# Window values for a chunked attention: a DRAM copy in padded groups of four rows, and a later query load

## The chip, the core and the metric

The kernel runs on one core of a Trainium2 chip. The core has five engines that run side by side and wait for each other through semaphores: TensorE (PE in the profile, with PEld for its weight loads), VectorE (DVE), ScalarE (ACT), GpSimd (POOL) and SyncE (SP). Transfers are issued by POOL, SP or ACT and are carried out by 16 DMA engines. The metric is the device time of one execution in microseconds (us), lower is better.

## The reference

Two stages. First a chunked attention over 4 batches, 8 heads, 768 positions and a head size of 64. Each chunk of 32 queries sees 8 memory rows and a window of 56 rows: 16 before the chunk, the chunk, 8 after it, cut at the ends of the sequence.

```python
for c in range(nc):                       # 24 chunks of 32
    l_start = max(0, c_start - 16); r_end = min(S, c_end + 8)
    k_full = concat([mem_k, k[:, :, l_start:r_end]], axis=2)
    v_full = concat([mem_v, v[:, :, l_start:r_end]], axis=2)
    a = softmax(scale * q[:, :, c_start:c_end] @ k_full.T)
    out[:, :, c_start:c_end] = a @ v_full
```

Then the 3072 rows of the result, 512 wide, go through a router with 8 experts: noisy logits, the two best experts for each row, softmax weights over these two, and for each chosen expert `relu(x @ w1[e]) @ w2[e]` with a hidden size of 1024, added up with its weight.

## The kernel before

The attention comes first, then the expert stage. The attention works batch by batch. A batch is three steps of 256 rows (`TP = 3`), so there are 12 steps (`NT`), step `i` belonging to batch `b = i // 3`.

For each batch the inputs come into SBUF by transfers that POOL issues (`load_nat`, line 117), which turn float32 into bfloat16 on the way. Row `p*6 + s` of a head lies on partition `p` in place `s`. From there:

- **Keys and queries** are turned by PE, two heads at a time (`turn`, line 393), into `kT` and `qT`. Four units turn the keys of a batch and four the queries. The units of the next batch are put between the steps of the present one by the table `PLAN`, queries first. DVE and ACT copy each result out of PSUM (line 531 for the first batch, 549 later).
- **Values** need another layout: PE wants, for each chunk, the 8 memory rows and the 56 window rows on 64 partitions, for even heads on partitions 0 to 63 and for odd heads on 64 to 127 (`vb`). Windows overlap and cross partitions, so the values take a way through DRAM. `spread_v` (line 368) lets POOL reorder `vn` into `vp`, in which a partition holds whole rows, the even heads before the odd ones. `window_v` then writes `vp` to the DRAM tile `vd` with one transfer that SP issues (line 374), and reads the windows back with four transfers that POOL issues (line 383): for each half of the heads the first 32 and the last 24 window rows. A partition of `vb` takes 24 pieces of 256 elements, one from each chunk. The memory rows come from `mvn` (line 378). `vd` has 16 rows of zeros before the sequence and 16 behind it, written at the start (line 156).

A step makes the scores (lines 408 and 415), subtracts the maximum (423, 425), takes the exponential on ACT (430), turns the probabilities (436, 439), multiplies with the values (453), divides by the sum (460), turns the rows for the router (470, 472) and makes the logits (480). The rows themselves go to the DRAM tile `xd`, one batch at a time, by a transfer that ACT issues (line 485; the last part by SP). The routing work of finished groups of rows lies between the steps on DVE, POOL and PE.

The order within PE, ACT, DVE and SP is the order of the program (`tc.manual_schedule`), and on POOL everything under `pin` keeps the order of the program too. Around the change POOL's order is: the loads of v, k, q of batch 0; constants; `spread_v(0)`; the memory rows and the window reads of batch 0; the loads of v, q, k of batch 1; `spread_v(1)`; the load of v of batch 2; the memory rows and window reads of batch 1; the loads of q and k of batch 2; and so on. A window read waits for the write of `vd`, and everything that POOL issues later waits behind it. After the window reads of the last batch come the loads of the first three experts.

The expert stage gathers rows from `xd` (line 671), makes the two products (lines 714 and 726), and scatters the sums to the output (line 677). It loads the other experts while it runs.

## Time and profile before

| what | value |
|---|---|
| median of 3 runs | 358.81 us (357.39 to 359.09) |
| the profiled execution | 358.42 us |
| its span, first to last instruction | 356.7 us |
| PE busy | 285.9 us (80%) |
| DVE busy | 170.3 us (48%) |
| ACT, POOL busy | 136.9 and 134.3 us |
| vd written, issue to landing (median of 4) | 9.0 us |
| window reads, issue to landing (median of 8 each) | 13.0 us (384 KB), 13.3 us (288 KB) |
| q, k, v loads, issue to landing (medians of 4) | 18.1, 20.9, 12.1 us |

The profiled time is the span plus 1.7 us around it. In the views, "L383" is line 383 of the kernel. A row of the timeline has the start and the length in us, engine, line, operation, result <- operands, the number of instructions, and in brackets how long the engine had been idle and for what. A row of a DMA queue has packets, MB and the time of its packets as a share of 16 engines; q0 carries what POOL issues, q1 what SP issues, q10 what ACT issues. Shares over 100% mean that packets of one engine overlap. "issue" in a wait means that the profile shows nothing that ended it.

### The profile page before, as it was taken

To read this page: it belongs to the slowest core of one execution; us is meant where nothing else is said; L and a number is where in the kernel's file an instruction comes from. 1 tells how busy PE (TensorE), PEld (TensorE's weight loads), DVE (VectorE), ACT (ScalarE), POOL (GpSimd) and SP (SyncE) were. 2 spreads that over 40 slices of the span, in tenths; PEclk is the share of its full clock that TensorE was granted. 3 is DMA by queue.
4 is the path that set the end of the run, shared out by engine and by line. 5 is a ranking of instruction groups with operands and counts; after the bars stand their busy time and mean duration, and the time that the engine had idled before them with its cause. 6 is when DMAs were issued, how large, how long until landed. Compare 5 with 4: busy or idle time off the path is not lost.

```text
span 356.7 us, 7042 instructions
## 1 busy us (share of the span) xinstructions
PE 285.9 (80%) x2934; PEld 186.3 (52%) x2955; DVE 170.3 (48%) x349; ACT 136.9 (38%) x189; POOL 134.3 (38%) x181
## 2 busy tenths in 40 slices
PE   0356577777847732999999999999999999999991
PEld 0245455666736621865544465664455775565540
DVE  7656456699689885531133302954310334223221
ACT  8813645564645610144322343213243222243310
POOL 6460573354453036706530744332580122201122
PEclk9995655565687865699999999999999999999998
DMA  8999999999999999499999999961289971100012
GB/s 122 235 171 169 245 174 208 251 198 211 247 156 208 253 249 180 106 194 143 178 196 235 209 173 252 159 119 51 87 166 189 208 184 54 53 2 2 25 47 81
DMA packets 49866, 56.97 MB, mean 160 GB/s; under 512 B 16931, under 2 KB 39523, under 8 KB 49828
## 3 DMA queue, kind: packets, MB, share of 16 engines
q0 software_dynamic: 34240, 46.82, 73.2%
q1 hardware_dynamic: 13920, 6.62, 10.9%
q10 hardware_dynamic: 1668, 3.02, 2.4%
q8 instruction: 25, 0.41, 0.5%
q14 instruction: 13, 0.11, 0.1%
HBM read 70.39 MB, written 13.96 MB: 236 GB/s over the span
## 4 chain that ended last, share of the span: by engine, by line
PE 33%; issue 20%; POOL 5%; DVE 4%; DMA 3%; POOLq 1%; ACT 0%; DVEq 0%
PE p_h L714 18%; PE p_y L726 13%; POOL out_dram L677 4%; DMA out_dram<-y,main_dst 1%; DMA xTt<-xt 1%; DMA xt<-xd,main_src 1%; POOL xt L671 1%; DVE w_all L460 1%; PE p_xt L691 0%; POOL w_all L844 0%; POOLq L981 0%; DVE mx L423 0%; DVE sc L425 0%; ACT xT L472 0%; PE ps_o L453 0%
## 5 line engine op out<-in xcount | busy, mean ns | idle before, releaser
L714 PE MATMUL p_h<-xTt,w_all 128*128 128x256 bf16 (+3 forms) x669 | 102.7, 313 | 0.7 <-DVE xTt L692 0.5
L726 PE MATMUL p_y<-w_all,h 128*128 128x512 bf16 x446 | 102.3, 379 | 0.9
L714 PEld LDWEIGHTS <-w_all 128*128 128x128 bf16 x736 | 70.0, 101 | 36.3 <-issue 0.7
L702 ACT ACTIVATE h<-p_h 128x512 bf16<-128x512 f32 (+1 forms) x81 | 44.7, 551 | 95.9 <-PE p_h L714 88.3
L726 PEld LDWEIGHTS <-h 128*128 128x128 bf16 x464 | 45.3, 98 | 51.6
L700 DVE TENSOR_SCALAR h<-p_h 128x512 bf16<-128x512 f32 (+1 forms) x49 | 31.0, 633 | 82.8 <-PE p_h L714 73.7
L677 POOL DMA_INDIRECT out_dram<-y,main_dst x28 | 30.9, 1103 | 87.9 <-DVE y L732 75.4
L732 DVE SCALAR_TENSOR_TENSOR y<-p_y,main_w,y 128x512 f32<-128x512 f32 x28 | 21.0, 750 | 39.2 <-PE p_y L726 32.5
L393 PE MATMUL p_t<-identb,w_all 128*64 128x128 bf16 x384 | 20.6, 288 | 23.0 <-DMA w_all<-in_k_dram 13.4
L671 POOL DMA_INDIRECT xt<-xd,main_src x28 | 27.9, 997 | 24.2 <-DMA xTt<-xt 13.0
L730 ACT ACTIVATE y<-p_y,main_w 128x512 f32<-128x512 f32 x28 | 19.2, 687 | 37.0 <-PE p_y L726 36.0
L393 PEld LDWEIGHTS <-w_all 128*64 128x64 bf16 x384 | 18.1, 155 | 25.2 <-DMA w_all<-in_k_dram 13.9
L439 ACT COPY pT<-p_p 128x1024 bf16<-128x1024 bf16 x12 | 12.1, 1012 | 27.5 <-PE p_p L436 27.5
L383 POOL DMA_DIRECT2D w_all<-vd x16 | 11.8, 747 | 23.8 <-DMA vd<-vp 19.3
L460 DVE TENSOR_TENSOR w_all<-ps_o,rs 128x512 bf16<-128x512 f32 x24 | 15.6, 686 | 8.2 <-PE ps_o L453 7.8
L415 PE MATMUL ps_s<-kT,qT 128*32 128x112 bf16 x384 | 11.6, 276 | 7.2 <-DVE kT L549 5.4
L368 POOL COPY vp<-w_all 128x1536 bf16<-128x1536 bf16 x8 | 11.5, 1469 | 13.2 <-DMA w_all<-in_v_dram 13.2
L430 ACT ACTIVATE pb<-sc 128x1024 bf16<-128x1024 f32 x12 | 12.8, 1063 | 8.9 <-DVE sc L425 8.7
L549 DVE COPY kT<-p_t 64x768 bf16<-64x768 bf16 x12 | 11.5, 955 | 7.9 <-PE p_t L393 7.8
L425 DVE TENSOR_TENSOR sc<-ps_s,mx 128x1024 f32<-128x1024 f32 x12 | 14.7, 1225 | 0.8
L423 DVE TENSOR_REDUCE mx<-ps_s 128x16 f32<-128x1024 f32 x12 | 14.7, 1224 | 0.8 <-PE ps_s L415 0.5
L453 PE MATMUL ps_o<-w_all,pT 128*32 128x128 bf16 x384 | 10.9, 280 | 3.3 <-issue 2.0
(172 smaller groups left out, 284.0 us busy)
## 6 DMA issues: line engine op xcount, KB each, us to landing
w_all<-in_moe_w_dram POOLq DMA_DIRECT2D x16, 1024.0 KB, 20.7
w_all<-in_moe_w_dram POOLq DMA_DIRECT2D x8, 512.0 KB, 13.8
w_all<-in_v_dram POOLq DMA_DIRECT2D x4, 768.0 KB, 12.1
w_all<-in_k_dram POOLq DMA_DIRECT2D x4, 768.0 KB, 20.9
w_all<-in_q_dram POOLq DMA_DIRECT2D x4, 768.0 KB, 18.1
vd<-vp SPq DMA_DIRECT2D x4, 768.0 KB, 9.0
w_all<-vd POOLq DMA_DIRECT2D x8, 384.0 KB, 13.0
w_all<-vd POOLq DMA_DIRECT2D x8, 288.0 KB, 13.3
```

The costliest lines, as they stand in the source:

```text
L393: nc.tensor.transpose(out=p_t[own(par), s, :], in_=src[:, 2 * pair + par, s * D:(s + 1) * D], identity=identb, tile_position=(0, par * 64))
L423: nc.vector.tensor_reduce(out=mx, in_=s3, axis=AX, op=Alu.max)
L425: nc.vector.tensor_tensor(out=sc, in0=s3, in1=bc(mx, KW), op=Alu.subtract)
L460: nc.vector.tensor_tensor(out=xr[:, j, 0:Dm].rearrange("p (h d) -> p h d", h=H), in0=ps_o[:, j].rearrange("p c a d -> p (c a) d"), in1=bc( ...
L671: i = nc.gpsimd.indirect_dma_start(out=xts[key].bitcast(I32), out_offset=None, in_=xd, in_offset=bass.IndirectOffsetOnAxis(ap=ix, axis=0))
L677: i = nc.gpsimd.indirect_dma_start(out=out, out_offset=bass.IndirectOffsetOnAxis(ap=ix, axis=0), in_=y, in_offset=None, bounds_check=N - 1 ...
L700: nc.vector.tensor_scalar(out=out_, in0=in_, scalar1=0.0, scalar2=None, op0=Alu.max)
L702: nc.scalar.activation(out=out_, in_=in_, func=Act.Relu)
L714: nc.tensor.matmul(out=o, lhsT=w(kp * F + f * 128, 128), rhs=x[:, kp], start=(kp == 0), stop=(kp == KP - 1))
L726: nc.tensor.matmul(out=p, lhsT=h[:, (f * n + j) * 128:(f * n + j + 1) * 128], rhs=w(KP * F + f * Dm, Dm), start=(f == 0), stop=(f == FB - 1))
L730: nc.scalar.activation(out=y, in_=p, func=Act.Copy, scale=weight)
L732: nc.vector.scalar_tensor_tensor(out=y, in0=p, scalar=weight, in1=y, op0=Alu.mult, op1=Alu.add)
```

## The change

1. `vd` gets another layout: 8 groups of 4 rows (row within a chunk = 4 g + k), and within a row first the half of the heads (`a`), then the chunk (25 of them, one more than the sequence has, for the window rows that reach over), then the 256 elements of a half row. A group is padded by 256 elements. So the pieces that one partition of `vb` takes lie behind each other in DRAM, 24 x 512 bytes = 12 KB. There are still four reads, now in the order: first 32 rows of the even and the odd heads, then last 24 rows of both.
2. The write of `vp` to `vd` becomes eight transfers on SP, each with 24 partitions and 8 pieces of 512 bytes from each.
3. The values are loaded and spread with 8 rows to a partition on 96 partitions, not 6 rows on 128.
4. The zeros become eight writes in place of four, and are issued behind the loads of the memory keys and values.
5. The queries of batch 0 are loaded behind `spread_v(0)` and ahead of its memory rows and window reads, not at the start.

```diff
@@ -105,26 +105,30 @@
         scol[0] -= n
         return wflat[:, scol[0]:scol[0] + n]
     xrow = [scratch(SO * Dm).rearrange("p (s r) -> p s r", s=SO) for _ in range(2)]
-    vn = scratch(H * SO * D).rearrange("p (h c) -> p h c", h=H)
+    SV = 8
+    VP = S // SV
+    vn = scratch(H * SV * D).rearrange("p (h c) -> p h c", h=H)
     vb = [scratch(2 * NCH * HP * D).rearrange("p (a c w) -> p a c w", a=2, c=NCH) for _ in range(2)][::-1]
     nat = [[scratch(H * SO * D).rearrange("p (h c) -> p h c", h=H) for _ in range(2)] for _ in range(2)]
     assert scol[0] >= 2 * WE
     mvs = w_all[0:B * NM, 0, 0:2 * H * D].bitcast(F32).rearrange("p (h d) -> p h d", h=H)
 
-    vd = [tc.dram_tile([S + CH, Dm], BF16, name=f"vd{i}") for i in range(2)]
+    VR = 4 * 2 * (NCH + 1) * HP * D
+    vd = [tc.dram_tile([CH // 4, VR + HP * D], BF16, name=f"vd{i}")[:, 0:VR].rearrange("g (k a c w) -> g k a c w", k=4, a=2, c=NCH + 1)
+          for i in range(2)]
 
     def load_nat(t, x, b):
         pin(nc.gpsimd.dma_start(out=t, in_=x[b].rearrange("h (p s) d -> p h (s d)", s=SO)))
 
     def load_v(b):
-        load_nat(vn, v, b)
+        pin(nc.gpsimd.dma_start(out=vn[0:VP], in_=v[b].rearrange("h (p s) d -> p h (s d)", s=SV)))
 
     def load_kq(b):
         for x in ((1, 0) if b else (0, 1)):
             load_nat(nat[b % 2][x], (k, q)[x], b)
 
     load_v(0)
-    load_kq(0)
+    load_nat(nat[0][0], k, 0)
 
     actx = ExitStack()
     keep = actx.enter_context(tc.tile_pool(name="keep", bufs=1))
@@ -147,21 +151,20 @@
     make_identity(nc, identb)
     identf = const.tile([NG, NG], F32, name="identf")
     nc.vector.tensor_copy(identf, identb[0:NG, 0:NG])
-    vp = keep.tile([128, H * SO * D], BF16, name="vp")
+    vp = keep.tile([128, SV * Dm], BF16, name="vp")
     lg_all = keep.tile([128, NG, 2 * E], F32, name="lg_all")
     zeros = keep.tile([128, Dm], BF16, name="zeros")
     nc.vector.memset(zeros, 0.0)
-    for i in range(2):
-        for r0, n in ((0, LC), (LC + S, CH - LC)):
-            nc.sync.dma_start(out=vd[i][r0:r0 + n, :], in_=zeros[0:n, :])
-
-
     mks = keep.tile([128, 2, D], F32, name="mks")
     nc.sync.dma_start(out=mks, in_=mem_k.rearrange("b h m d -> (b h m) d").rearrange("(x p) d -> p x d", p=128))
     mkn = keep.tile([128, 2, D], BF16, name="mkn")
     nc.vector.tensor_copy(mkn, mks)
     for b in range(B):
         nc.sync.dma_start(out=mvs[b * NM:(b + 1) * NM], in_=mem_v[b].rearrange("h m d -> m h d"))
+    for i in range(2):
+        for g0, c in ((0, 0), (LC // 4, NCH)):
+            for a in range(2):
+                nc.sync.dma_start(out=vd[i][g0:g0 + LC // 4, :, a, c], in_=zeros[0:LC, 0:HP * D])
     mvn = keep.tile([B * NM, Dm], BF16, name="mvn")
     wgs = keep.tile([128, KP, 2 * E], F32, name="wgs")
     nc.scalar.dma_start(out=wgs[:, :, 0:E], in_=moe_w_gate.rearrange("(kp p) e -> p kp e", p=128))
@@ -366,22 +369,25 @@
     def spread_v(b):
         for par in range(2):
             pin(nc.gpsimd.tensor_copy(
-                out=vp.rearrange("p (s a c d) -> p a c s d", s=SO, a=2, c=HP)[:, par],
-                in_=vn.rearrange("p (c a) (s d) -> p a c s d", a=2, s=SO)[:, par]))
+                out=vp.rearrange("p (s a c d) -> p a c s d", s=SV, a=2, c=HP)[0:VP, par],
+                in_=vn.rearrange("p (c a) (s d) -> p a c s d", a=2, s=SV)[0:VP, par]))
 
     def window_v(b):
         t, o = vb[b % 2], vd[b % 2]
-        nc.sync.dma_start(out=o[LC:LC + S, :].rearrange("(p s) c -> p (s c)", s=SO), in_=vp)
+        for x in range(CH // SV):
+            c0, g = divmod(LC // SV + x, CH // SV)
+            for z in range(2):
+                nc.sync.dma_start(out=o[2 * g + z, :, :, c0:c0 + NCH].rearrange("k a c w -> c (k a) w"),
+                                  in_=vp[x:VP:CH // SV, z * 4 * Dm:(z + 1) * 4 * Dm].rearrange("p (s w) -> p s w", w=HP * D))
         for par in range(2):
             p0 = par * 64
             cols = slice(par * 256, (par + 1) * 256)
             pin(nc.gpsimd.dma_start(out=t[p0:p0 + NM, par], in_=mvn[b * NM:(b + 1) * NM, cols].unsqueeze(1).to_broadcast([NM, NCH, 256])))
-        for par in range(2):
-            p0 = par * 64
-            cols = slice(par * 256, (par + 1) * 256)
-            for r0, n in ((0, CH), (CH, WIN - CH)):
-                pin(nc.gpsimd.dma_start(out=t[p0 + NM + r0:p0 + NM + r0 + n, par],
-                                        in_=o[r0:r0 + S, cols].rearrange("(c k) w -> k c w", k=CH)[0:n]))
+        for x, n in ((0, CH), (1, WIN - CH)):
+            for par in range(2):
+                p0 = par * 64 + NM + x * CH
+                pin(nc.gpsimd.dma_start(out=t[p0:p0 + n, par].rearrange("k c w -> k (c w)"),
+                                        in_=o[0:n // 4, :, par, x:x + NCH].rearrange("g k c w -> g k (c w)")))
 
 
     def turn(b, unit):
@@ -525,6 +531,7 @@
             nc.vector.memset(vb[0][own(par), 1 - par], 0.0)
         nc.vector.tensor_copy(mvn.rearrange("m (a c d) -> m a c d", a=2, c=HP), mvs.rearrange("m (c a) d -> m a c d", a=2))
         spread_v(0)
+        load_nat(nat[0][1], q, 0)
         window_v(0)
         for u in range(2 * HP):
             for o_, i_ in turn(0, u):
```

## The prediction

> **What bounds the kernel now.** I read the span first, then the page's slices of the span.
>
> ```profile
> core 0: 356.7 us, clock 0.867
> PE   0356577777847732999999999999999999999991
> DVE  7656456699689885531133302954310334223221
> DMA  8999999999999999499999999961289971100012
> ```
>
> A slice is 8.9 us. From slice 17 on (about 144 us) PE is full: that is the expert stage, and its end moves with its start. Before that, in the attention, no compute engine is full, and the DMA engines are. The change lies wholly in that first stretch, so the question is which transfers PE waits for there. PE's rows in order of time say it (start, length, what it idled for):
>
> ```profile
> 20.33 2.77 PE L393 MATMUL p_t<-identb,w_all 128*64 128x128 bf16 x48 [3.03 <-DMA w_all<-in_q_dram]
> 32.79 1.04 PE L453 MATMUL ps_o<-w_all,pT 128*32 128x128 bf16 x32 [1.30 <-DMA w_all<-vd]
> 39.77 2.43 PE L393 MATMUL p_t<-identb,w_all 128*64 128x128 bf16 x48 [1.25 <-DMA w_all<-in_q_dram]
> 45.62 2.13 PE L393 MATMUL p_t<-identb,w_all 128*64 128x128 bf16 x36 [3.43 <-DMA w_all<-in_k_dram]
> 61.15 1.04 PE L453 MATMUL ps_o<-w_all,pT 128*32 128x128 bf16 x32 [2.03 <-issue]
> 68.03 1.49 PE L393 MATMUL p_t<-identb,w_all 128*64 128x128 bf16 x24 [2.63 <-DMA w_all<-in_q_dram]
> 98.57 1.46 PE L393 MATMUL p_t<-identb,w_all 128*64 128x128 bf16 x36 [1.44 <-DMA w_all<-in_k_dram]
> ```
>
> The last window read of batch 1 is issued at 47.97 us; its row among the DMA issues ends in the time to landing:
>
> ```profile
> w_all<-vd POOLq DMA_DIRECT2D x1, 288.0 KB, 12.9
> ```
>
> So after the first batch has started, PE loses 1.30 + 1.25 + 3.43 + 2.03 + 2.63 + 1.44 = 12.1 us to late transfers. The row at 61.15 is such a wait too, although it says "issue": the read landed at 47.97 + 12.9 = 60.9 us. All of these transfers are issued by POOL and land one behind the other, so what one of them costs is passed to the next. DVE decides how much of a removed PE wait reaches the end:
>
> ```profile
> 47.16 3.88 DVE L549 COPY kT<-p_t 64x768 bf16<-64x768 bf16 x4 [7.55 <-PE p_t L393]
> 62.25 1.29 DVE L460 TENSOR_TENSOR w_all<-ps_o,rs 128x512 bf16<-128x512 f32 x2 [2.83 <-PE ps_o L453]
> 69.86 0.26 DVE L457 RECIPROCAL rs<-small 128x16 f32<-128x16 f32 x1 [1.04 <-PE small L447]
> 101.77 3.87 DVE L549 COPY kT<-p_t 64x768 bf16<-64x768 bf16 x4
> ```
>
> At 47 and 62 us DVE was idle for longer than PE's wait; at 69.86 for 1.04 us; at 101.77 not at all.
>
> **What the transfers cost.** Rows of the DMA view for six stretches (packets, MB, share of 16 engines). 32 to 39 us, only loads of q, k, v:
>
> ```profile
> q0 software_dynamic: 1867, 1.41, 130.8%
> ```
>
> 52 to 54 us, only window reads, and 22 to 23 us, their beginning in batch 0:
>
> ```profile
> DMA packets 101, 0.33 MB, mean 164 GB/s; under 512 B 21, under 2 KB 21, under 8 KB 101
> q0 software_dynamic: 101, 0.33, 98.9%
> ```
> ```profile
> DMA packets 67, 0.25 MB, mean 254 GB/s; under 512 B 5, under 2 KB 5, under 8 KB 67
> ```
>
> 16 to 18 us, mostly the write of vd; 2 to 3 us, small starting loads; 62 to 64 us, three queues at once:
>
> ```profile
> DMA packets 234, 0.77 MB, mean 385 GB/s; under 512 B 2, under 2 KB 124, under 8 KB 234
> q1 hardware_dynamic: 110, 0.68, 84.7%
> ```
> ```profile
> q1 hardware_dynamic: 355, 0.09, 38.4%
> ```
> ```profile
> q10 hardware_dynamic: 73, 0.45, 54.2%
> q1 hardware_dynamic: 56, 0.29, 36.9%
> q0 software_dynamic: 68, 0.05, 16.6%
> ```
>
> A load packet takes 7 us x 16 engines / 1867 = 60 ns; the 1024 of a q or k load, 64 to an engine, 3.85 us. The window reads of a batch, 2 x 384 and 2 x 288 KB = 1.38 MB, run at 164 GB/s with the engines full: 8.4 us, about 9 with their gaps. The vd write (6 KB runs) has 0.847 x 32 us / 110 = 246 ns a packet, 2.0 us for 128 packets on 16 engines. A small packet of the SP queue (256 B, 2 to 3 us) takes 0.384 x 16 us / 355 = 17 ns. When three queues are busy they pass about equally many packets (73, 56, 68).
>
> **The change, part by part.**
>
> *Window reads (L383).* Every partition now reads one run of 12 KB in place of 24 runs of 512 B. Bounds: 9.0 us a batch as now, and 1.38 MB at 385 GB/s, 3.6 us. I take 4.6 us (300 GB/s): above the 254 of their best stretch and below the 385 of the 6 KB runs, because each DMA still writes 32 or 24 partitions and that row serves 128. Saved: 4.4 us a batch on the queue that everything waits for. The Trainium skill, SBUF — State Buffer, section "Can I just issue two DMAs to hit both halves?", says that two transfers to the two halves of the partitions serialize; by the 218 GB/s that the page gives for 32 partitions the reads would take an estimate of 6.3 us, and no run here shows it.
>
> *vd write (L374).* One DMA with 128 packets of 6 KB becomes eight of 24 x 8 = 192 packets of 512 B: 1536 packets. Price of one: 17 ns for 256 B plus 256 B more at 246 ns per 6 KB (10 ns) = 28 ns, so 2.7 us a batch over 16 engines in place of 2.0: +0.7. Bounds: 2.0 us (the bytes alone) and 60 ns, the load packet, 5.8 us. I take 28, because a plain HW packet is nearer to the HW rows. The Trainium skill, DMA: Bandwidth & Descriptors, "Why a DMA increments its semaphore by 16 and not by 1", says that 24 rows would use 12 engines only; by that it would be an estimate of 3.6 us, and no run here shows the engines. More important is the sharing: at one packet each in turn, 96 write packets beside load packets last 96 x 88 ns = 8.4 us, so vd lands later when loads are queued, while the loads lose only the 2.7 us.
>
> *Eight issues on SP.* An issue takes 0.3 to 0.4 us:
>
> ```profile
> 12.51 68.06 SPq L374 DMA_DIRECT2D vd<-vp  x4
> 127.02 0.32 SPq L485 DMA_DIRECT2D xd<-w_all  x1
> 9.62 2.87 POOL L368 COPY vp<-w_all 128x1536 bf16<-128x1536 bf16 x2 [2.83 <-DMA w_all<-in_v_dram]
> 13.65 1.36 POOL L378 DMA_DIRECT2D w_all<-mvn  x2 [1.17 <-DVE mvn L526]
> 19.97 2.96 POOL L383 DMA_DIRECT2D w_all<-vd  x4 [4.95 <-DMA vd<-vp]
> ```
>
> Eight are about 3 us; SP has nothing else between the four writes and 127 us, so only vd's landing feels it. The eight zero writes (four before) go behind mem_k and mem_v, 3 us before the first spread ends: nothing.
>
> *spread_v (L368).* 96 partitions x 2048 elements a copy in place of 128 x 1536: 2.87 x 4/3 = 3.83 us, +1.0 a batch. It is hidden behind the queue of loads in batches 1 to 3 and on the path in batch 0. While POOL copies (77.34 to 80.2), one DVE row takes 2.49 us that elsewhere takes 0.19:
>
> ```profile
> 77.34 2.88 POOL L368 COPY vp<-w_all 128x1536 bf16<-128x1536 bf16 x2
> ```
> ```profile
> 77.77 2.49 DVE L307 TENSOR_TENSOR facts<-ii 128x6 bf16<-128x6 f32 x1
> 105.67 0.19 DVE L307 TENSOR_TENSOR facts<-ii 128x8 bf16<-128x8 f32 x1
> ```
>
> So a copy that is 1.0 us longer can hold DVE up to 1 us longer in the batch where DVE is full; or nothing, if the copy moves off it. I take nothing and keep 1 us for the range.
>
> *v load*: the same bytes in 768 runs of 2 KB in place of 1024 of 1.5 KB: nothing, as the loads already move 1.41 MB of bf16 in 7 us, 201 GB/s, and twice that in f32.
>
> *q of batch 0.* Its issue goes from 3.45 us to behind the spread: 9.62 + 3.83 = 13.5, data from about 15.3 (an estimate: 0.9 us to issue it and as much to start). Its 64 packets an engine now share with the vd write: 64 x 88 ns = 5.6, plus 0.8 to be reported: 21.7 us in place of 20.3. The first scores slip by 1.4 us. The constants that it is moved behind on POOL merely start 0.9 us earlier. vd lands when both are through, 15.3 + 3.85 + 2.7 + 0.8 = 22.6 (19.9 before). The mvn rows (L378) and the reads stand behind it on POOL; the reads start at 24.0 and end at 28.6 in place of 32.7. Behind them on POOL and in the queue are v, q, k of batch 1, so all of these come about 4 us earlier, less 0.7 for the longer vd write beside k and 0.3 for gaps: k at 42.5 instead of 45.6, 3.1 us.
>
> *The sum.* The 1.4 us of the start is taken up by the waits of 1.30 and 1.25 that vanish. k of batch 1: 3.1 us, in full, as DVE idled 7.55. Windows of batch 1: by then two read savings less two longer writes; they end about 55, PE is ready for them at 59.1 - 3.1 = 56: the wait of 2.03 goes, DVE idled 2.83. q of batch 2: the 2.63 goes, but DVE gives back only its 1.04 and a bit: 1.2. k of batch 3: 1.44 on PE, nothing, DVE was busy. Late next is DVE, which from 66 us on has few gaps. Sum 3.1 + 2.0 + 1.2 = 6.3 us. The profiled execution took 358.42 us (span 356.7), 0.4 below the median of the runs, 358.81: 352.1 there, 352.5 as a median.
>
> **The rivals.** A measurement of this kernel tells about 0.5% (1.8 us) from no change.
>
> 1. *Reads half mended.* Each DMA fills only 32 or 24 partitions and they follow each other at half of the 385 GB/s: 7.1 us, 1.9 saved a batch. Reads of batch 0 end at 31.1, k of batch 1 gains 0.6, the windows 1.8, q 0.8: 3.2, so 355.6 us. For it: 4 KB read packets at 164 GB/s with full engines do not look like a cost per run. Against it: 254 GB/s for 1 us. The Trainium skill's page named at the reads speaks for this one.
> 2. *Reads as slow as now* (the length of the run was never the limit): 9.0 us. In batch 0 they end at 33.0, 0.3 late, and with the longer write k of batch 1 is 1.3 late: 360.1. Against it as above.
> 3. *The small writes are dear* (slower). At 60 ns a packet q of batch 0 lands at 15.3 + 64 x 120 ns + 0.8 = 23.8 and vd at 15.3 + 3.85 + 5.8 + 0.8 = 25.8, the reads end at 31.8, and k of batch 1, beside 5.8 us of writes (3.8 more), lands 32.7 - 31.8 - 3.8 - 0.3 = 3.2 late. With 0.5 more in the next batches, 362.5 us. It decides from the packet price p at which 32.7 - (25.9 + 96 p) and the rest, 192 p in all against 8.45 us, cancel: 44 ns. Against it: 17 ns at 256 B.
> 4. *ACT is held* (slower). ACT issues the write of xd itself:
>
> ```profile
> 57.76 0.37 ACTq L485 DMA_DIRECT2D xd<-w_all  x1
> 50.96 0.91 POOL L117 DMA_DIRECT2D w_all<-in_k_dram  x1 [1.32 <-DMA w_all<-in_v_dram]
> vd<-vp SPq DMA_DIRECT2D x4, 768.0 KB, 9.0
> ```
>
> The second row shows an issue that waits for an earlier, unrelated load to land. With eight writes in place of one, the xd issue could come to wait for one of them, 9.0 us from issue to landing, some 6 us after ACT gets there, in one batch, and 2 in the next: 358.8 - 6.3 + 8 = 360.5 or more. Against it: the order of the issues may stay as it is, xd first.
>
> **How the numbers follow.** Forecast 0.47 (own range 349 to 356); rival 1 0.13 (355.6); rival 2 0.14 (360.1); rival 3 0.19 (362.5); rival 4 0.07 (360.5). Faster: 0.47 + 0.13 = 0.60; same: rival 2 and a little of the others, 0.16; slower: 0.24. The range goes from 348.5 (reads at their lower bound, 1 us a batch more, and the 2.63 and 1.44 of PE counted in part) to 362.5, which holds the rivals but for the worse half of the third; the 1 us of DVE lies inside.
>
> **What would show it.** Right: 12 KB or 4 KB read packets with a DMA rate near 300 GB/s or more in a stretch of reads only; SP's small packets at some 28 ns; the first q rows of PE near 21.7 and those of k of batch 1 near 42.5; no PE wait before L453 near 56. Wrong: a write packet of 45 ns or more, a q row past 23 us, a read rate still at 164, ACT idle before L485.

## The result and the profile after

The changed kernel takes 371.44 us (median of 4 runs, 369.12 to 372.46) against 358.91 us for the kernel before beside it (357.39 to 359.09): ratio 1.035, 95% interval 1.0293 to 1.0406. It is 12.5 us slower; 352.5 us was predicted, at most 362.5. The profiled execution took 372.46 us, its span 370.9. Here and below a ratio counts the runs of a kernel that lie within 1.5% of its fastest; where that leaves many out, the ratio of the medians of all runs stands beside it.

From the page of the changed kernel: the slices of the DMA engines, the groups of the window reads and of the spread (busy us, mean ns of one | idle time before them and what ended it), and the issues of the write (32 in place of 4).

```profile
DMA  8879995995996999969999999961169992100012
...
L389 POOL DMA_DIRECT2D w_all<-vd x16 | 8.7, 551 | 54.1 <-DMA vd<-vp 53.9
L371 POOL COPY vp<-w_all 96x2048 bf16<-96x2048 bf16 x8 | 14.9, 1904 | 12.1 <-DMA w_all<-in_v_dram 12.1
vd<-vp SPq DMA_DIRECT2D x32, 96.0 KB
```

The row of nines in the DMA slices has holes now (5 and 6). POOL stood 53.9 us at the four batches' window reads, waiting for the write of `vd`. The same wait among POOL's waits in the kernel before (us in total, times, longest) was 19.3 us in three batches. For the reads of batch 1 the view names no cause for the 4.4 us that POOL idled before them; with these it is 23.7.

```profile
POOL w_all L383 <- DMA vd<-vp: 19.3, 3, 8.9
```

SP's issues of the write, with their shortest, median and longest duration in ns and their first and last start, in the kernel before and in the changed one:

```profile
L374 SPq DMA_DIRECT2D vd<-vp x4: 319/334/355, 12.5 to 80.2; - x4
```
```profile
L380 SPq DMA_DIRECT2D vd<-vp x32: 750/753/2898, 13.8 to 101.2; - x32
```

PE's rows in order of time answer to those of the prediction:

```profile
23.17 2.77 PE L399 MATMUL p_t<-identb,w_all 128*64 128x128 bf16 x48 [5.46 <-DMA w_all<-in_q_dram]
36.04 1.04 PE L459 MATMUL ps_o<-w_all,pT 128*32 128x128 bf16 x32 [1.71 <-DMA w_all<-vd]
47.36 1.20 PE L399 MATMUL p_t<-identb,w_all 128*64 128x128 bf16 x36 [1.15 <-DMA w_all<-in_k_dram]
69.97 1.04 PE L459 MATMUL ps_o<-w_all,pT 128*32 128x128 bf16 x32 [9.62 <-DMA w_all<-vd]
80.95 2.13 PE L399 MATMUL p_t<-identb,w_all 128*64 128x128 bf16 x36 [1.96 <-DMA w_all<-in_k_dram]
96.45 0.63 PE L459 MATMUL ps_o<-w_all,pT 128*32 128x128 bf16 x32 [2.43 <-DMA w_all<-vd]
109.60 1.20 PE L399 MATMUL p_t<-identb,w_all 128*64 128x128 bf16 x36 [3.11 <-DMA w_all<-in_k_dram]
157.04 1.86 PE L721 MATMUL p_h<-xTt,w_all 128*128 128x128 bf16 x16 [0.52 <-DVE xTt L699]
```

The last row is the first product of the expert stage; before, it stood at 144.14:

```profile
144.14 1.86 PE L714 MATMUL p_h<-xTt,w_all 128*128 128x128 bf16 x16 [0.52 <-DVE xTt L692]
```

So 12.9 of the 14.2 us by which the span grew were lost ahead of the expert stage. The windows of batch 0 were 3.2 us late (36.04 against 32.79), those of batch 1 already 8.8 (69.97 against 61.15), and the largest single wait, 9.62 us, stands there.

What POOL did about the reads of batches 1 and 2 shows how the wait is passed on (start, length, idle time before):

```profile
26.97 2.17 POOL L389 DMA_DIRECT2D w_all<-vd  x4 [10.96 <-DMA vd<-vp]
44.42 1.31 POOL L385 DMA_DIRECT2D w_all<-mvn  x2
58.39 1.64 POOL L389 DMA_DIRECT2D w_all<-vd  x3 [12.66 <-DMA vd<-vp]
60.86 0.96 POOL L121 DMA_DIRECT2D w_all<-in_q_dram  x1
87.40 2.17 POOL L389 DMA_DIRECT2D w_all<-vd  x4 [18.56 <-DMA vd<-vp]
```

The load of q of batch 2 (60.86), and that of k behind it, stand behind the reads. In four stretches just ahead of the reads the DMA engines had nothing left to do; columns are the window, its length, PE, PEld, DVE, ACT and POOL busy, PE's clock, DMA share, GB/s:

```profile
26.00:28.20 2.20, 1.47 (x45) 1.18 (x43) 1.21 (x3) 0.14 (x1) 1.23 (x3) 1.00 0.00 0
56.50:59.60 3.10, 3.10 (x64) 2.73 (x64) 2.95 (x5) 1.12 (x2) 1.21 (x3) 0.50 0.02 3
86.60:88.60 2.00, 2.00 (x36) 1.83 (x28) 1.39 (x2) 0.52 (x1) 1.20 (x3) 0.50 0.01 0
111.20:113.40 2.20, 1.59 (x28) 1.14 (x28) 2.15 (x4) 2.15 (x3) 1.18 (x3) 0.50 0.00 0
```

### The profile page after: what moved, and what is told of

Its sections match the earlier page's. It is cut to its first block, busy times and chain, and to the rows that moved or that the text cites. A ratio compares the mean times of both kernels' runs of the same rounds, so it can differ in the third digit from the quotient of the medians.

```text
span 370.9 us, 7112 instructions
## 1 busy us (share of the span) xinstructions
PE 284.3 (77%) x2955; PEld 183.8 (50%) x2955; DVE 172.7 (47%) x349; ACT 136.7 (37%) x189; POOL 134.7 (36%) x181
## 3 DMA queue, kind: packets, MB, share of 16 engines
q1 hardware_dynamic: 19904, 6.62, 10.8%
## 4 chain that ended last, share of the span: by engine, by line
PE 32%; issue 19%; POOL 5%; DVE 3%; DMA 3%; POOLq 1%; ACT 1%; DVEq 0%; ACTq 0%
PE p_h L721 17%; PE p_y L733 13%; POOL out_dram L684 3%; DMA out_dram<-y,main_dst 1%; POOL xt L678 1%; DMA xTt<-xt 1%; DVE w_all L466 1%; DMA xt<-xd,main_src 1%; PE p_xt L698 0%; PE p_list L355 0%; POOLq L988 0%; POOL w_all L851 0%; ACT xT L478 0%; ACT pT L445 0%; PE p_p L442 0%
## 5 line engine op out<-in xcount | busy, mean ns | idle before, releaser
L733 PE MATMUL p_y<-w_all,h 128*128 128x512 bf16 x464 | 103.7, 379 | 0.0
L399 PE MATMUL p_t<-identb,w_all 128*64 128x128 bf16 x384 | 19.7, 277 | 26.1 <-DMA w_all<-in_k_dram 16.1
L399 PEld LDWEIGHTS <-w_all 128*64 128x64 bf16 x384 | 17.0, 147 | 28.1 <-DMA w_all<-in_k_dram 16.8
L389 POOL DMA_DIRECT2D w_all<-vd x16 | 8.7, 551 | 54.1 <-DMA vd<-vp 53.9
L466 DVE TENSOR_TENSOR w_all<-ps_o,rs 128x512 bf16<-128x512 f32 x24 | 15.5, 686 | 15.4 <-PE ps_o L459 14.8
L459 PE MATMUL ps_o<-w_all,pT 128*32 128x128 bf16 x384 | 9.6, 258 | 14.9 <-DMA w_all<-vd 13.8
L371 POOL COPY vp<-w_all 96x2048 bf16<-96x2048 bf16 x8 | 14.9, 1904 | 12.1 <-DMA w_all<-in_v_dram 12.1
L436 ACT ACTIVATE pb<-sc 128x1024 bf16<-128x1024 f32 x12 | 12.8, 1064 | 13.8 <-DVE sc L431 13.7
L431 DVE TENSOR_TENSOR sc<-ps_s,mx 128x1024 f32<-128x1024 f32 x12 | 14.7, 1225 | 0.8
L429 DVE TENSOR_REDUCE mx<-ps_s 128x16 f32<-128x1024 f32 x12 | 14.7, 1223 | 0.7 <-PE ps_s L421 0.4
L556 DVE COPY kT<-p_t 64x768 bf16<-64x768 bf16 x12 | 11.5, 954 | 7.5 <-PE p_t L399 7.4
L459 PEld LDWEIGHTS <-pT 128*32 128x32 bf16 x384 | 7.3, 114 | 15.3 <-issue 15.1
## 6 DMA issues: line engine op xcount, KB each, us to landing
w_all<-in_v_dram POOLq DMA_DIRECT2D x4, 768.0 KB, 10.6
```

Of the source, the lines that this page charges most:

```text
L371: pin(nc.gpsimd.tensor_copy(out=vp.rearrange("p (s a c d) -> p a c s d", s=SV, a=2, c=HP)[0:VP, par], in_=vn.rearrange("p (c a) (s d) -> p ...
L399: nc.tensor.transpose(out=p_t[own(par), s, :], in_=src[:, 2 * pair + par, s * D:(s + 1) * D], identity=identb, tile_position=(0, par * 64))
L459: nc.tensor.matmul(out=ps_o[r * CH:(r + 1) * CH, j, pair], lhsT=pT[:, j * HP + pair, r * CH:(r + 1) * CH], rhs=vb[b % 2][:, :, (tp * 2 + j ...
L466: nc.vector.tensor_tensor(out=xr[:, j, 0:Dm].rearrange("p (h d) -> p h d", h=H), in0=ps_o[:, j].rearrange("p c a d -> p (c a) d"), in1=bc( ...
L733: nc.tensor.matmul(out=p, lhsT=h[:, (f * n + j) * 128:(f * n + j + 1) * 128], rhs=w(KP * F + f * Dm, Dm), start=(f == 0), stop=(f == FB - 1))
```

## The experiments

The theory at the start, W: the write in eight transfers of small packets lands late, POOL stands at the window reads meanwhile, and the load queue behind POOL runs dry. The rival, Q: the later queries of batch 0 are the loss. The experiments ran on other chips than the result, where the kernel before took 360 to 364 us, so ratios against that kernel on the same chip are compared, and beside them the start of the first p_h row (the attention's end, 157.04 above). That row is of one execution of each kernel. All times are of kernels that differ from the changed kernel or from the kernel before by the edit named; of longer edits the main lines are shown.

### The parts alone: queries, write, number of issues

Queries of batch 0 at the start again, everything else as changed:

```diff
-    load_nat(nat[0][0], k, 0)
+    load_kq(0)
...
-        load_nat(nat[0][1], q, 0)
```

> The changed kernel with the queries of batch 0 loaded at the start again; all else stays changed. Theory W (the vd write lands late, because its 1536 small packets take turns with the queued loads, POOL stands at the window reads until it has landed, and behind POOL the load queue runs dry): the start gains 1 to 3 us, the later batches stay as they are: 368 to 371 us. Rival Q (the late queries and the dead time they leave at the start are the loss): 361 us or less.

Measured: 370.72 us, ratio 1.0221 [1.0158, 1.0284], first p_h row 153.90. So the layout with its write loses 2.2% without the queries' part.

The other way round, the kernel before with nothing but the later queries:

```diff
-    load_kq(0)
+    load_nat(nat[0][0], k, 0)
...
         spread_v(0)
+        load_nat(nat[0][1], q, 0)
```

> The kernel before with only the queries of batch 0 moved behind the spread. Theory W: they land 2 to 3 us later and most of it is met again in the waits for the windows and the next keys: 359 to 361.5 us. Rival Q: 367 us or more.

Measured: 363.54 us, ratio 1.0018 [0.9981, 1.0055]. Batch 0's first q row starts at 23.50 us there, 3.2 later than in the kernel before, and the end does not feel it. Alone, the later queries are not the cause. To the changed kernel they add what lies between 1.0221 and 1.035, about 1.3% (the two ratios are from different chips), 3.1 us in the first p_h row.

The changed kernel with the copy written by one transfer of 96 runs of 8 KB, with late and with early queries:

```diff
-        for x in range(CH // SV):
-            c0, g = divmod(LC // SV + x, CH // SV)
-            for z in range(2):
-                nc.sync.dma_start(out=o[2 * g + z, :, :, c0:c0 + NCH].rearrange("k a c w -> c (k a) w"),
...
+        nc.sync.dma_start(out=vflat[b % 2][0:S * Dm].rearrange("(p c) -> p c", p=VP), in_=vp[0:VP])
```

(`vflat` is the tile of `vd` as one row.)

> The changed kernel with vd written by one transfer of 96 runs of 8 KB a batch, and the zeros by one for the unwritten rest: the window reads keep their 12 KB runs and byte count but find the values in the wrong places, so the attention computes on misplaced values. Theory W: the write is back at 2 us of engine time and lands in 7 to 10 us, so the time falls below the kernel before, 352 to 357 us. Rival Q: 364 us or more, since the start is untouched. If the reads on their few partitions are the loss: 367 or more.

> The one-write kernel (vd written by one transfer of 8 KB runs, so the values lie in wrong places and the attention computes on them) with the queries of batch 0 loaded at the start again. What is left of the change is the 96-partition values and the reads with 12 KB runs. If the 12 KB reads save 4 us of queue a batch as the prediction took, and only the late queries hid it: ratio to the kernel before 0.975 to 0.99. If the reads save engine time but land no earlier, because they lie on few engines each: 0.995 to 1.01.

Measured: 366.03 us, ratio 1.0084 [1.0042, 1.0127], with late queries; 360.8 us, ratio 0.9826 [0.977, 0.9881] (medians of all runs: 0.992), with early ones. POOL's wait at the reads in the second one's page, and its first p_h row:

```profile
L385 POOL DMA_DIRECT2D w_all<-vd x16 | 8.7, 551 | 20.7 <-DMA vd<-vp 18.9
```
```profile
143.69 1.86 PE L716 MATMUL p_h<-xTt,w_all 128*128 128x128 bf16 x16 [0.51 <-DVE xTt L694]
```

The wait is back at 18.9 us. How much the reads gain is less sure. The ten runs with early queries spread from 354.83 to 364.58 us, and the ratio 0.9826 (6.3 us) rests on the four lowest of them; by the medians of all runs the gain is 2.9 us (360.8 against 363.69). In the row, runs in the layout before on the same chip stood at 146.95 (spread on 96 partitions, below) and 148.18 (late queries), 3.3 and 4.5 us behind; this profiled execution took 364.12 us, above its median. So the gain of the reads is 3 to 6 us. With late queries the expectation of W, 352 to 357 us, failed: 366.03 lies in Q's range. Beside a large write the later queries cost about what the reads gain. From large write to small packets, the same row goes from 143.69 to 153.90, 10.2 us.

The kernel before with its write, still in 6 KB packets, cut into eight transfers:

```diff
-        nc.sync.dma_start(out=o[LC:LC + S, :].rearrange("(p s) c -> p (s c)", s=SO), in_=vp)
+        for p in range(0, 128, 16):
+            nc.sync.dma_start(out=o[LC + p * SO:LC + (p + 16) * SO, :].rearrange("(p s) c -> p (s c)", s=SO), in_=vp[p:p + 16])
```

> The kernel before with its vd write cut into eight transfers of 16 partitions, the packets still 6 KB. If the eight issues on SP, some 0.4 us each, make the write late: ratio 1.01 or more. If it is the 512-byte packets that take turns with the loads: within 0.5% of the kernel before.

Measured: 367.84 us, ratio 1.0118 [1.0034, 1.0202]. Eight issues have a price of their own, without small packets: POOL stood 44.9 us at the reads (23.7 before), and the first p_h row came at 154.03, 6 to 7 us behind the two rows named above and as late as that of the changed kernel with early queries. SP's waits show one reason: in the middle of a batch's eight it stood for an unrelated transfer of ACT's.

```profile
POOL w_all L384 <- DMA vd<-vp: 44.9, 4, 14.4
```
```profile
SPq L375 <- DMA xd<-w_all: 15.6, 2, 9.0
```

Four transfers of 16 pieces in place of eight of 8, without padding, queries early:

```diff
-            for z in range(2):
-                nc.sync.dma_start(out=o[2 * g + z, :, :, c0:c0 + NCH].rearrange("k a c w -> c (k a) w"),
-                                  in_=vp[x:VP:CH // SV, z * 4 * Dm:(z + 1) * 4 * Dm].rearrange("p (s w) -> p s w", w=HP * D))
+            nc.sync.dma_start(out=o[2 * g:2 * g + 2, :, :, c0:c0 + NCH].rearrange("g k a c w -> c (g k a) w"),
+                              in_=vp[x:VP:CH // SV].rearrange("p (s w) -> p s w", w=HP * D))
```

> The changed kernel with queries early, without padding, and the copy written by four transfers of 24 partitions with 16 runs of 512 B, instead of eight with 8 runs: the same packets in half as many issues. Theory W in the form that the packets' turns beside the loads are the cost: first to last write packet still 10 to 15 us, ratio 1.02 to 1.04. If the number of issues is the cost (each waits for earlier ones to land): first to last 5 to 8 us, ratio 1.00 to 1.01.

Measured: 370.91 us, ratio 1.0313 [1.0196, 1.043] (medians of all runs: 1.024); the write's packets of batch 1 took 9.9 us from first to last, of batch 2 14.8. Half the issues mend nothing.

Half the values in 512-byte packets, half in 4 KB runs, eight transfers:

```diff
+        for g in range(4):
+            nc.sync.dma_start(out=vt[b % 2][2 * g + 1, 0:S * Dm // 8].rearrange("(p c) -> p c", p=VP // 4),
+                              in_=vp[g * VP // 4:(g + 1) * VP // 4, 4 * Dm:8 * Dm])
```

> The changed kernel with batch 0's queries loaded at the start, eight writes a batch as in the changed kernel, but four of them carry half of the values in 512 B packets (768 a batch instead of 1,536) and four carry the other half in 96 runs of 4 KB, to other places (those values come to lie in wrong places of the copy, so attention works on misplaced values). If the number of small packets sets the write's length: first to last write packet 6 to 8 us instead of 11 to 15, ratio between the runs with all small and with one large write, 1.000 to 1.010. If it is the eight issues: as with all small, 1.015 to 1.025. If the load queue bridges a write of 7 us without running dry: 0.98 to 0.99.

Measured: 371.61 us, ratio 1.0236 [1.0129, 1.0343], first p_h row 152.58; 10 to 13 us from first to last write packet. Half the small packets cost as much as all of them. Neither the number of issues nor the number of packets alone sets the loss. The small-packet transfers of these two runs have 24 rows each, like those of the changed kernel.

### What else was new: spread, padding, where the transfers are issued

The values loaded and spread on 96 partitions, rows unpadded as before, one large write, reads in 512-byte pieces:

```diff
+        nc.sync.dma_start(out=o[LC // 4:(LC + S) // 4, :].rearrange("(p z) r -> p z r", z=SV // 4),
+                          in_=vp[0:VP].rearrange("p (z r) -> p z r", z=SV // 4))
...
+                pin(nc.gpsimd.dma_start(out=t[p0:p0 + n, par],
+                                        in_=o[x * CH // 4:x * CH // 4 + S // 4].rearrange("(c g) (k a w) -> g k a c w", g=CH // 4, k=4, a=2)[0:n // 4, :, par]))
```

> The values' loading and spread on 96 partitions alone: values are loaded and spread as in the changed kernel (96 partitions, eight rows each), but the DRAM copy has rows of all heads one behind the other without padding, is written by one transfer of 96 runs of 8 KB, and is read in 512 B pieces; batch 0's queries are loaded at the start. Theory W (the slow write in eight transfers of 512 B packets holds POOL at the reads and the load queue runs dry) makes this the kernel before in all that counts: ratio 0.995 to 1.010, write first to last packet 3 to 6 us, reads 12 to 15 us a batch. Rival S (the spread on 96 partitions, 1.9 us a call instead of 1.4, and the v load of 96 partitions are themselves dear): ratio 1.02 or more with the same waits.

Measured: 364.05 us, ratio 1.0043 [1.0, 1.0087]. Load and spread on 96 partitions cost next to nothing.

One large write, early queries, no padding:

```diff
-    vt = [tc.dram_tile([CH // 4, VR + HP * D], BF16, name=f"vd{i}") for i in range(2)]
+    vt = [tc.dram_tile([CH // 4, VR], BF16, name=f"vd{i}") for i in range(2)]
```

> One large write as in the earlier run of that kind, queries early, but no padding behind each group of four rows (the reads' 32 or 24 partitions are then one even stride). The values come to lie in wrong places of the copy, so attention works on misplaced values; the work in time is the same. If the gain of 1.7% came from the 12 KB runs alone: ratio 0.977 to 0.990, reads 6 to 8 us a batch. If the padding (the split into groups of four rows, and so the spread over the engines) is what makes the reads fast: reads 10 us or more, ratio 0.995 to 1.005.

Its whole time, 1174 us, tells nothing of the attention: with these misplaced values the expert stage runs far longer. The first line of its page and its first p_h row:

```profile
span 1168.0 us, 12986 instructions
```
```profile
144.25 1.87 PE L716 MATMUL p_h<-xTt,w_all 128*128 128x128 bf16 x16 [0.51 <-DVE xTt L694]
```

Up to that row it is the padded one (143.69) within 0.6 us; the reads of its four batches took 7.6, 12.8, 16.0 and 15.2 us from first to last packet, the padded ones 6.8, 10.6, 12.7 and 10.2. So the long runs make the gain in the row. The padding shortens the reads, but by that row little comes of it.

Loads of keys and queries moved ahead of the window reads on POOL, to keep the queue filled:

```diff
+        if between is not None:
+            between()
         for x, n in ((0, CH), (1, WIN - CH)):
...
-                window_v(b + 1)
-                if b + 2 < B:
-                    load_kq(b + 2)
+                window_v(b + 1, (lambda: load_kq(b + 2)) if b + 2 < B else None)
```

> The changed kernel with POOL issuing the key and query loads of the batch after next ahead of the window reads, so that the load queue is not empty while POOL waits for the vd write. Theory W: two empty stretches of 3 to 5 us of the DMA engines vanish, 362 to 366 us, but the write, which now always has company, lands later still. Rival Q: no change, 370 to 372. If only the landing of the write counts and not the empty queue: 371 or more.

Measured: 375.45 us, ratio 1.0247 [1.0152, 1.0342] (medians of all runs: 1.036): not clearly better than 1.035, and not the 362 to 366 us of W. Its PE waits, in an execution of 377.19 us:

```profile
PE ps_o L461 <- DMA w_all<-vd: 24.6, 3, 15.9
```

The filled queue pushed the write back: first to last packet 20.8 us in batch 1, where the changed kernel had 12.3.

The window reads issued by SP, in the kernel before and in the changed kernel with early queries:

```diff
-                pin(nc.gpsimd.dma_start(out=t[p0 + NM + r0:p0 + NM + r0 + n, par],
+                nc.sync.dma_start(out=t[p0 + NM + r0:p0 + NM + r0 + n, par],
```

> The kernel before with the window reads issued by SP, so that POOL no longer stands behind the vd write and the loads of the next batches are queued without a pause. If POOL standing there costs time in the kernel before too: ratio 0.98 to 0.995. The rival: the load queue of the kernel before never runs empty, so nothing is won, and the reads with 512-byte packets now take turns with the loads and land later: 1.00 to 1.02.

> The changed kernel with the queries of batch 0 at the start and the window reads issued by SP behind the eight writes. If the empty load queue behind POOL's wait is what the slow write costs: ratio 0.99 to 1.01, against 1.022 with the reads on POOL. If it is the late landing of the values themselves: 1.02 or more.

Measured: 376.57 us, ratio 1.0357 [1.028, 1.0434], and 388.19 us, 1.0645 [1.0535, 1.0755]. The first is slower than either theory had it; the second lies where the late landing was to put it. With POOL free to load ahead, the reads are what comes late. PE's waits for the windows, first in the kernel before with its reads on SP, then in the changed one:

```profile
PE ps_o L453 <- DMA w_all<-vd: 25.7, 3, 12.8
```
```profile
PE ps_o L459 <- DMA w_all<-vd: 42.4, 4, 19.8
```

The eight writes issued by POOL, behind the loads in one queue:

```diff
-                nc.sync.dma_start(out=o[2 * g + z, :, :, c0:c0 + NCH].rearrange("k a c w -> c (k a) w"),
+                pin(nc.gpsimd.dma_start(out=o[2 * g + z, :, :, c0:c0 + NCH].rearrange("k a c w -> c (k a) w"),
```

> The changed kernel with batch 0's queries loaded at the start, the eight writes of the values' copy issued by POOL (behind the loads of the next batch in POOL's own queue) instead of by SP. Theory W, in the form that the write is slow because its 512 B packets take turns with the loads' packets on another queue: in one queue they follow each other, first to last write packet 3 to 6 us instead of 11 to 15, the engines stand empty for 2 to 4 us a batch at most, PE's waits for the windows shrink to below 3 us, ratio 0.98 to 1.00. Rival N (512 B write packets are dear wherever they are queued): first to last 10 us or more, ratio 1.02 to 1.04 as with SP. Rival I (the issuing of eight such transfers is the cost): POOL busy 0.7 to 1.5 us more for each, 6 to 12 us a batch, ratio 1.03 or more.

Measured: 371.9 us, ratio 1.0302 [1.0228, 1.0377]. POOL's rows for batch 1:

```profile
42.37 4.34 POOL L380 DMA_DIRECT2D vd<-vp  x7
50.37 0.62 POOL L380 DMA_DIRECT2D vd<-vp  x1 [3.67 <-DMA w_all<-in_v_dram]
53.90 2.18 POOL L389 DMA_DIRECT2D w_all<-vd  x4 [1.65 <-DMA vd<-vp]
```

The wait at the reads is short now (1.65 us here), but POOL spends 11.5 us from the first write to the first read, and the loss is the same. Another queue is no cure. In the trace these writes are 192 packets of 4 KB a batch and not 1536 of 512 bytes, so this run does not test small packets in one queue.

### Taking the loss apart: packets or standing?

Reads that need not wait, because they take the input of the values in place of the copy:

```diff
-                                        in_=o[0:n // 4, :, par, x:x + NCH].rearrange("g k c w -> g k (c w)")))
+                                        in_=v[b].rearrange("h s d -> (h s d)").rearrange("(r c) -> r c", c=NCH * HP * D)[par * CH:par * CH + n]))
```

> The changed kernel with batch 0's queries loaded at the start, where the window reads (same number, same 12 KB runs, same destinations) take their data from the input of the values instead of from the copy, so that POOL need not wait for the copy's write. The eight writes of 512 B packets are still made, beside the loads as before. Values come to lie in wrong places of the windows (attention works on misplaced values), so the MoE's lists differ a little; the start of the MoE's first p_h row is compared beside the time. Theory W (POOL stands at the reads, the load queue runs dry): without the wait the attention is back at what one large write gave, first p_h row at 142 to 147 us and ratio 0.975 to 0.995. Rival B (1,536 small packets a batch beside the loads take the loads' time, waiting or not): first p_h row at 151 to 155 us, ratio 1.01 to 1.03.

Measured: 384.88 us, ratio 1.0599 [1.0518, 1.0681], first p_h row 166.39. Neither theory had this. POOL's wait had only moved, to the next spread, which needs `vp` free:

```profile
POOL vp L371 <- DMA vd<-vp: 51.5, 3, 18.6
```

With the queue full the write took 26 to 28 us from first to last packet in batches 0 to 2. Three stretches of the DMA view, each with a write of the same 0.79 MB (q1) beside loads (q0; packets, MB, share of 16 engines): 46.5 to 74.5 us of this kernel, 45 to 57.5 us of the changed kernel, 40 to 45 us of the kernel before.

```profile
q0 software_dynamic: 2886, 3.71, 84.0%
q1 hardware_dynamic: 1632, 0.79, 14.5%
```
```profile
q0 software_dynamic: 1116, 1.13, 57.6%
q1 hardware_dynamic: 1632, 0.79, 26.2%
```
```profile
q0 software_dynamic: 758, 0.57, 79.0%
q1 hardware_dynamic: 144, 0.79, 38.3%
```

In the changed kernel the write is done after 12 us; the loads beside it run out on the way, and none of them is a read of the input in 12 KB packets, as 112 of the 2886 are.

The same with two `vp` in turn, so that nobody waits for the write, and without the writes:

```diff
-    vp = keep.tile([128, SV * Dm], BF16, name="vp")
+    vps = [vp0, keep.tile([128, SV * Dm], BF16, name="vp")]
```

> As the run whose window reads take the input, and the eight writes a batch are left out altogether (nothing of the values' copy is written but its zero rows; attention works on misplaced values). This is what is left of the changed kernel without the write. If the write is the whole loss: first p_h row at 138 to 145 us, ratio 0.955 to 0.985. If something else in the changed kernel is slow (the reads of 12 KB runs beside the loads, the spread on 96 partitions): first p_h row at 148 us or more, ratio above 1.0.

> As the run whose window reads take the input, with the eight writes of 512 B packets a batch, and with two buffers for the spread values in turn, so that POOL waits for the write neither at the window reads nor at the next spread (it waited 51.5 us at the spread there); attention works on misplaced values. Theory W (the cost is POOL's standing, the packets beside the loads cost little): first p_h row at 138 to 147 us and within 3 us of the run without the writes, ratio 0.96 to 0.99. Rival B (the small packets take the loads' time, turn by turn, waiting or not): first p_h row at 150 us or later, 8 us or more behind the run without the writes, ratio 1.01 or more.

Measured: without writes 356.59 us, ratio 0.9791 [0.9705, 0.9878], first p_h row 139.86; with writes that nobody waits for 365.65 us, ratio 1.0077 [1.0029, 1.0125], row at 148.56. The writes cost 8.7 us though nobody waits for them, so W, in which they cost little, falls in this form; the row itself lies between the ranges of W and B. But these reads were of float32 input, turned into bfloat16 on the way. In the trace their packets have 12 KB, not about 1 KB as the next text has it, but one takes about 1 us, where those of the changed kernel take 0.6 to 0.8. Hence the last pair, with reads of a small bf16 copy:

```diff
-                                        in_=v[b].rearrange("h s d -> (h s d)").rearrange("(r c) -> r c", c=NCH * HP * D)[par * CH:par * CH + n]))
+                                        in_=vz[0:n // 2].unsqueeze(1).to_broadcast([n // 2, 2, NCH * HP * D])))
```

> In the two runs before, the window reads took the input, which is float32 and is turned into bfloat16 on the way; so they were not the 12 KB runs that their expectations named, but packets of about 1 KB. Here the reads take a small bf16 copy (16 rows of 12 KB, written once, in batch 0, by one transfer of 24 runs of 8 KB; two partitions share a row), so they are 12 KB runs and wait for nothing after batch 0. The eight writes a batch in 512 B packets are made, from two buffers in turn, and nobody waits for them. Attention works on misplaced values. If POOL's standing is about half of the loss, as the run with two buffers suggests: first p_h row 4 to 7 us ahead of the changed kernel with early queries (153.90), 147 to 150. If it is the whole loss: at 144 or before. If the packets alone are the loss: at 152 or later.

> As the run with the small copy, without the eight writes (attention works on misplaced values). First p_h row at 135 to 140 us, since the run without writes and with slow reads was at 139.86. Its distance to the run with the writes is the price of 1,536 small packets a batch that nobody waits for: 2.7 us a batch by the price of 28 ns a packet on 16 engines, 10.8 us in all; 7 to 10 us by the distance of the two runs before (8.7). Its distance to the kernel with one large write and early queries (143.69) is the whole price of a large write, wait included: 4 to 8 us.

The expert stage again ran over a millisecond with these values, so only the part up to the first p_h row counts. With writes, without writes:

```profile
149.35 1.86 PE L726 MATMUL p_h<-xTt,w_all 128*128 128x128 bf16 x16 [0.52 <-DVE xTt L704]
```
```profile
135.65 1.86 PE L721 MATMUL p_h<-xTt,w_all 128*128 128x128 bf16 x16 [0.52 <-DVE xTt L699]
```

This divides the attention's end, with early queries: 135.65 with no write; 143.69 with one large write and its wait (+8.0); 149.35 with small packets that nobody waits for (+13.7, where 7 to 10.8 was expected); 153.90 with small packets and POOL standing at the reads (another 4.6). So of the 10.2 us between large write and small packets, at least 5.7 are what the write takes from the loads, and up to 4.6 POOL's standing. The division is rough. Each row is of one execution, the last pair ran on a chip whose kernel before took 359.65 us, 0.7 to 1.1% less than beside the other two, and the pair before it has the write at 8.7 us in place of 13.7. Each share may be off by some 2 us, the first by more.

No version with all values in their places beat the kernel before.

## Why the prediction was wrong, step by step

*What bounds the kernel* was read rightly: transfers in the attention; 12.9 of the 14.2 us of the span lie there.

*Window reads: right in kind, priced too well.* From issue to PE, batch 0: 19.97 to 32.79 before, 12.8 us; 26.97 to 36.04 after, 9.1. Saved 3.8 us (4.4 predicted). Their packets took 7.2, 9.1, 7.0 and 6.7 us from first to last in the four batches, not 4.6. Rival 1 had 7.1, but counted its gain from 9.0 us where the kernel before took 12.8 from issue to use. With one large write the reads gained 3 to 6 us at the end. The Trainium skill's rule for the two halves of the partitions (SBUF — State Buffer, "Can I just issue two DMAs to hit both halves?"), by which 6.3 us was estimated, is nearer to the trace's 7 us than the forecast was.

*vd write, its own time: about right.* 28 ns a packet was taken, 10.8 us for four batches on 16 engines. The two pairs of runs with and without the small packets give 8.7 and 13.7 us, 23 and 36 ns a packet. The large write cost 8.0 us for four, the 2.0 us a batch predicted, but with its waits in it. By the second pair the extra is 5.7 us in place of 2.8; the first pair has no run with a large write.

*vd write, its landing: the step that failed.* "At one packet each in turn, 96 write packets beside load packets last 96 x 88 ns = 8.4 us, so vd lands later when loads are queued, while the loads lose only the 2.7 us" was worked out for batch 0 and then dropped: for batch 1 the prediction has "two read savings less two longer writes; they end about 55", as if POOL had not to wait for that landing. PE had the windows of batch 1 at 69.97. Spread 1 ended at 43.4 us, the write landed at 58.4, and POOL, with the loads of q and k of batch 2 behind it, stood until then (12.66 us), while the queue emptied (56.5 to 59.6). By the division above, this standing is up to 4.6 us of the loss.

The 8.4 us were too short as well, by the number of engines and by the length of a turn. The 1632 packets of a batch's write are 1536 of data and 96 more, 12 for each of the eight transfers; the large write's 144 are 128 and 16. That agrees with the rule of the Trainium skill, DMA: Bandwidth & Descriptors, "Why a DMA increments its semaphore by 16 and not by 1", by which 24 rows use 12 engines. Then an engine has 136 of the packets and not 96. The stretch of 70 to 76 us, batch 2's write beside a full load queue, gives the turn:

```profile
q0 software_dynamic: 1209, 0.93, 98.7%
q1 hardware_dynamic: 665, 0.32, 27.2%
```

On twelve engines that is a write packet in 6 us x 12 / 665 = 108 ns, where 88 was taken. 136 x 108 ns = 14.7 us is an estimate from these rows; the write took 15.4 us from first to last packet. In the 28 us shown above, whose loads include the 12 KB reads, a turn took 206 ns in the same way.

*Eight issues: wrong in size.* 0.3 to 0.4 us was taken from an issue of 128 long runs; one of 24 x 8 short ones took 0.75, some up to 2.9. Eight lasted 9.6 and 10.3 us in batches 0 and 1 and 6.5 in batch 2, not 3. That "only vd's landing feels it" was true and mattered.

*Rival 3, dear small writes,* had the right sign. Its threshold of 44 ns was too high, since POOL's standing was left out of batches 1 to 3; at 23 to 36 ns the kernel already lost.

*q of batch 0: too cheap in company.* The q row was predicted at 21.7 and came at 23.17, past the mark of 23 that the prediction named as wrong. By itself the move cost nothing (1.0018), with the slow write about 1.3%, with one large write 1.8% by the medians of all runs (366.03 of 362.24 us against 360.8 of 363.69). The wait of 1.30 us that was to vanish and take it up is still there, 1.71 us at 36.04.

*Spread, v load, zeros: right.* Two copies of 1904 ns, 3.81 us a batch (3.83 predicted), and nothing measurable at the end (1.0043). *Rival 4:* ACT was not held; it was SP that stood for ACT's transfer, and only in runs with eight issues (0.2 us in the changed kernel itself).

*What stays open.* The parts measured do not quite make up the whole: 10.2 us for the write and 3.1 for the later queries, less 3 to 6 for the reads, are 7 to 10 of the 12.9 us, from rows of different chips.

Open too is how even the turns are. The Trainium skill, DMA: Bandwidth & Descriptors, "Queues, rings and completion order", says that each engine takes a packet of each queue in turn. In 70 to 76 us even turns would pass 665 load packets on the write's twelve engines, and the four others 400 more at 60 ns each; by this estimate 1065 pass, and 1209 did. So even turns come near, but the trace does not name the engine of a packet. Pauses of SP are not needed for a late landing. In batch 2 the eight issues followed each other without one, and that write was the longest of the four:

```profile
66.47 6.50 SPq L380 DMA_DIRECT2D vd<-vp  x8
```

No run sent the small packets over all 16 engines, so what the use of twelve costs is not shown. That four issues and half the packets changed nothing would fit a write that lands whenever the loads run out, but this was only argued.

## What to carry to other kernels

A layout that turns many short reads into long ones turns the long writes into short ones if both sides cut the data differently; price the write's landing beside a full load queue, on the engines that its rows reach, and not only its bytes. Carry such a landing through every batch, and ask at each what stands behind the engine that waits for it. Here reads that gained 3 to 6 us cost 10 us on the side of the write.

## What the runs showed that was not expected

Alone, 512-byte write packets are quick. In the changed kernel, 24 to 25 us, when all loads were through:

```profile
q1 hardware_dynamic: 513, 0.25, 86.0%
```

That is 513 packets in a us, 27 ns each by their share (0.86 x 16 us / 513), the price predicted; beside loads 58 to 130 a us went through. Next, a wait taken away made the kernel slower (1.0221 to 1.0599) where it only moved to the next spread. The likely reason is that POOL's standing had held back the loads, which let the write through; this was not shown by itself, since those reads of the input also took 12 to 13 us a batch in place of 7 to 9. With two buffers, where the wait was gone, the ratio was 1.0077. And SP's issues can stand for transfers that ACT issued (15.6 us in two waits), although neither touches the other's data: in the trace SP's transfer waits for the completion semaphore that ACT's transfer had used, 110 and then 112, and sets the same one.
